# A third raw place and five float32 places for the weight halves of a two-expert kernel

## The chip, the cores and the metric

The kernel runs on one core of one Trainium2 chip. The metric is the device time of one execution in microseconds (us).

## The reference

Three steps follow each other. An attention over q, k and v of 4 batches, 8 heads, 576 rows and 64 columns keeps, in each row of scores, only those within tau of the row's maximum, and softmaxes them. Its output, 2304 rows of 512, goes through a first expert, whose activation is a quotient of polynomials, and the result through a second one, whose activation is piecewise quadratic:

```
attn = softmax(where(scores >= max(scores) - tau, scores, -1e9))
x  = (attn @ v) as 2304 x 512
h  = x @ w_in                      # 512 x 2048
g  = (a0 + a1 h + a2 h^2 + a3 h^3) / (1 + |b0||h| + |b1| h^2 + 1e-6)
x  = g @ w_out                     # 2048 x 512
h  = x @ w2_in
g  = h if h >= 1, 0 if h <= -1, else (h + 1)^2 / 4
out = g @ w2_out
```

The four weight matrices are handed over as float64; q, k, v and the output are float32.

## The kernel before, in words

All large products are done in float16 with the operands split in a high and a low part (three matmuls for one product). The work goes batch by batch: attention of a batch, first expert (24 steps: 3 blocks of 192 rows x 8 chunks of 256 of the 2048 columns), second expert (24 steps), then the next batch. `at(when)` (L175) gives each piece of work a priority, lowest first; a scheduler with a simulated time line makes each engine's order from it, when the program is built. A tile's place (a pool's tag has so many) is given out in that schedule, and is free when the last reader of the tile in it is done.

**Weights.** Each expert has 8 chunks with 2 halves each (x = 0: 512 x 256 of w_in; x = 1: 256 x 512 of w_out), 32 halves in all; they are numbered here from 0 to 31 in program order, the first expert's from 0 to 15. `convert` (L233) handles one half:
- L241 loads the raw half, 1 MB of float64 seen as pairs of int32, on the SP queue into a tile with the tag "rw" (pool rp, 2 places).
- `as_float` (L220) builds the float32 half in a tile "wt" (N_WT = 3 places, 4 KB in a partition) with three passes on DVE, L228, L229 and L230.
- L253 makes Gram products of the half on PE, L254 and L188 find their maximum (with matmuls of L187 between), and L168 to L172 a power of two from it.
- `split` (L205) scales the float32 half on ACT (L217), casts it to float16 (L208, the high part) and subtracts on POOL in four pieces (L212, the low part). The subtraction is the last reader of the float32 half.

For the first expert the two parts go into the chunk's own tile "wc" (8 places), which stays for the first batch, and a copy into DRAM scratch (L265). For the second expert they go through a staging tile "wh" (N_WH = 2 places, 4 KB in a partition) into scratch (L270); load_chunk (L275) reads chunks back later. The first expert's halves are interleaved with the first batch's attention (L869 to L875), the second expert's have the priorities of steps -3 to 17 (WEIGHTS, L887). The first expert's constants need a maximum over all of its halves.

**Attention of the first batch** (`first_attention`, L619) works on 4 pairs of heads. `prep_pair` (L317) loads raw q and k of one pair into the tile "rqk" (pool rp, 1 place, 5 KB in a partition), squares it on ACT for a bound (L328), scales and splits it into the float16 tile "qk" (pool ap, 1 place, 4.5 KB in a partition; for the first batch L217, L208, L212, for the others L214 and L215), and transposes that by DMA (L343 or L350). All four pairs are prepared by about 97 us. The next pair that uses these two tiles is the first of batch 1 (`attention`, L461; priority of step 16.5 on). Its v (`prep_v`, L289) is loaded into "rw" tiles, L300 and L298.

SP carries nearly all DMAs, in the order of the schedule.

Of the kernel before, what the change touches and what calls it, by code (L numbers as in the profile page):

```python
# [11 lines left out]
I32 = mybir.dt.int32  # L12
BF16 = mybir.dt.bfloat16
AF = mybir.ActivationFunctionType
ALU = mybir.AluOpType
# [19 lines left out]
N_TEMP, N_POLY, N_WT, N_WH, N_GG, N_ROW, N_SC = 5, 3, 3, 2, 4, 3, 2  # L35


ATTENTION = {1: (18, 50), 2: (60, 100), 3: (108, 147)}
WEIGHTS = (0, 20)

# [2 lines left out]
def tile_attention_moe_moe2(  # L43
# [18 lines left out]
    V, A, G, T, Q = nc.vector, nc.scalar, nc.gpsimd, nc.tensor, nc.sync  # L62
    B, H, S, D = q.shape
    P = 128
# [4 lines left out]
    DM, DF = w1_in.shape  # L69
    KT = DM // P  # L70
    NCH = 8
    CF = DF // NCH
    NF = CF // P
# [5 lines left out]
    E = KT * CF  # L79
# [3 lines left out]
    rp = ctx.enter_context(tc.tile_pool(name="rp", bufs=2))  # L83
    ap = ctx.enter_context(tc.tile_pool(name="ap", bufs=2))
    xp = ctx.enter_context(tc.tile_pool(name="xp", bufs=1))
    mp = ctx.enter_context(tc.tile_pool(name="mp", bufs=2))
# [106 lines left out]
    wide = w1_in.dtype != F32  # L193
    words = 2 if wide else 1
# [22 lines left out]
            A.activation(src, src, AF.Copy, scale=scale)  # L217
            split(hi, lo, src)

    def as_float(raw, name):  # L220

        if not wide:
            return raw
        src = raw.rearrange("p (n w) -> p n w", w=2)
        t = mp.tile([P, E], I32, name="wt" + name, tag="wt", bufs=N_WT)
        V.tensor_scalar(t, src[:, :, 1], 0x07FFFFFF, 3, op0=ALU.bitwise_and, op1=ALU.logical_shift_left)  # L228
        V.scalar_tensor_tensor(t, src[:, :, 1], -0x40000000, t, op0=ALU.bitwise_and, op1=ALU.bitwise_or)  # L229
        V.scalar_tensor_tensor(t, src[:, :, 0], 29, t, op0=ALU.logical_shift_right, op1=ALU.bitwise_or)  # L230
        return t.bitcast(F32)

    def convert(m, i, x, dst, on_vector):  # L233

        if x == 0:
            raw = rp.tile([P, KT, CF * words], raw_type, name=f"rw{m}_{i}_0", tag="rw")
            src = w_in_dram[m][:, i * CF * words : (i + 1) * CF * words].rearrange("(kt p) f -> p kt f", p=P)
        else:
            raw = rp.tile([P, NF, DM * words], raw_type, name=f"rw{m}_{i}_1", tag="rw")
            src = w_out_dram[m][i * CF : (i + 1) * CF, :].rearrange("(f p) d -> p f d", p=P)  # L240
        Q.dma_start(raw, src)  # L241
        name = f"{m}_{i}_{x}"
        src = as_float(raw.rearrange("p a b -> p (a b)"), name)
        hi, lo = dst[:, 0:E], dst[:, E : 2 * E]
        columns = m == 0 and x == 0
        bound = gram[:, i : i + 1] if columns else small(1, "mb" + name)
# [711 lines left out]
```

## Time and profile before

| | us |
|---|---|
| median of 3 runs | 1245.84 |
| lowest, highest | 1241.46, 1250.6 |
| the profiled execution | 1242.5 |
| its span | 1240.7 |
| PE busy in it (matmuls) | 1091.9 (88%) |
| DVE busy | 977.1 (79%) |
| ACT busy | 842.9 (68%) |
| POOL busy | 543.0 (44%) |
| mean granted clock of PE | 0.959 |

PE is the matmul engine, PEld its weight load, DVE the vector engine, ACT the scalar engine, POOL GpSimd, SP the queue that issues DMAs. Times are counted from the start of the span. A name such as wt<-rw says that a tile wt is written from a tile rw; L228 is line 228. In a time line each row is start, duration, engine, line, operation, tiles and shapes, with the idle time of the engine before it and what ended that in brackets.

### The profile page before, as it was taken

The numbers are of one execution on the slowest core, as the hardware profiler recorded it, in microseconds if no ns is written. First come the engines' busy times: TensorE is split into PE (matmuls) and PEld (weight loads), VectorE is DVE, ScalarE is ACT, GpSimd is POOL, SyncE is SP. The second block draws the span as 40 slices with busy tenths as digits, with TensorE's granted clock in tenths as the row PEclk, the third lists the DMA queues.
The fourth block names the chain that finished last, engine by engine and source line by source line (L and its number), as shares of the span: only waits on it lengthen the run. The fifth ranks groups of instructions, "written<-read, shape, count | busy, mean of one in ns | idle before, by whom it ended". The sixth has DMA issues, their size and how long they took to land.

```text
span 1240.7 us, 31727 instructions
## 1 busy us (share of the span) xinstructions
PE 1091.9 (88%) x12618; PEld 984.5 (79%) x12618; DVE 977.1 (79%) x2353; ACT 842.9 (68%) x1533; POOL 543.0 (44%) x700
## 2 busy tenths in 40 slices
PE   2787788588799999999888998998899999999998
PEld 1444455488688888899788898998788989999997
DVE  7767887899997777799997776899996768896431
ACT  2477776779785677777875776887766767775332
POOL 3424545675673556421464555223563653222221
PEclk9797898799899999999999999999999999999999
DMA  7656676734447465923596539513993478007000
GB/s 209 230 169 217 218 258 205 240 116 120 108 136 234 68 125 116 249 73 92 144 238 131 110 69 245 140 49 68 243 192 69 86 167 221 14 1 259 16 14 27
DMA packets 220341, 176.40 MB, mean 142 GB/s; under 512 B 182048, under 2 KB 193312, under 8 KB 212000
## 3 DMA queue, kind: packets, MB, share of 16 engines
q1 hardware_dynamic: 220192, 174.36, 52.7%
q8 instruction: 99, 1.62, 0.5%
q14 instruction: 50, 0.41, 0.1%
HBM read 106.83 MB, written 21.50 MB: 103 GB/s over the span
## 4 chain that ended last, share of the span: by engine, by line
PE 35%; DVE 19%; DMA 9%; ACT 6%; POOL 6%; issue 6%; SPq 1%; DVEq 0%; ACTq 0%; POOLq 0%
PE ph L843 15%; PE acc L857 15%; DMA eT<-hl 7%; POOL hl L395 3%; DVE e L384 2%; PE pv L410 2%; DVE t L731 2%; DVE t L726 2%; DVE sc L422 2%; DVE t L737 1%; DMA qkT<-qk 1%; DVE t L728 1%; POOL gg L212 1%; DVE t L727 1%; ACT hl L392 1%
## 5 line engine op out<-in xcount | busy, mean ns | idle before, releaser
L857 PE MATMUL acc<-gg,wc 128*128 128x192 f16 x4608 | 427.6, 247 | 9.8 <-POOL gg L212 6.4
L843 PEld LDWEIGHTS <-wc 128*128 128x128 f16 x4608 | 389.8, 99 | 37.4 <-issue 20.8
L857 PEld LDWEIGHTS <-wc 128*128 128x128 f16 x4608 | 383.4, 98 | 13.3 <-issue 12.0
L212 POOL TENSOR_TENSOR gg<-t,gg 128x384 f16<-128x384 f32 x192 | 193.3, 1008 | 380.0 <-ACT gg L208 330.0
L843 PE MATMUL ph<-xT,wc 128*128 128x192 f16 x2304 | 220.2, 253 | 29.7 <-DVE t L728 21.2
L843 PE MATMUL ph<-yT,wc 128*128 128x192 f16 x2304 | 215.9, 247 | 1.0 <-DVE rk_f L160 0.6
L395 POOL TENSOR_TENSOR hl<-e,hl 128x256 f16<-128x256 f32 x216 | 154.3, 735 | 0.0
L208 ACT CAST gg<-t 128x384 f16<-128x384 f32 x192 | 97.0, 508 | 68.8 <-DVE t L790 34.7
L789 DVE SCALAR_TENSOR_TENSOR t<-t,c 128x384 f32<-128x384 f32 x96 | 64.0, 667 | 77.3 <-ACT t L788 77.0
L384 DVE SCALAR_TENSOR_TENSOR e<-sc,nt,e 128x576 f32<-128x576 f32 x108 | 96.2, 891 | 31.9 <-ACT e L383 31.3
L393 POOL TENSOR_TENSOR hl<-e,hl 128x64 f16<-128x64 f32 x108 | 43.3, 401 | 145.0 <-ACT hl L392 141.4
L788 ACT ACTIVATE t<-ph,c 128x384 f32<-128x384 f32 x96 | 64.0, 667 | 51.6 <-PE ph L843 51.2
L383 ACT ACTIVATE e<-sc,nt,con 128x576 f32<-128x576 f32 x108 | 93.4, 865 | 7.4 <-POOL hl L395 1.3
L410 PE MATMUL pv<-v,eT 128*128 128x65 f16 (+3 forms) x1680 | 70.1, 194 | 26.8 <-DMA eT<-hl 26.6
L422 DVE TENSOR_SCALAR_CACHE_REDUCE sc<-s 128x576 f32<-128x576 f32 x108 | 80.9, 749 | 13.5 <-PE s L377 12.7
L410 PEld LDWEIGHTS <-eT 128*128 128x128 f16 (+1 forms) x1680 | 62.2, 100 | 36.1 <-DMA eT<-hl 33.8
L724 ACT ACTIVATE t<-ph,sc 128x384 f32<-128x384 f32 x96 | 55.2, 575 | 51.5 <-PE ph L843 50.0
L392 ACT CAST hl<-e 128x576 f16<-128x576 f32 x108 | 72.0, 668 | 25.9 <-DVE e L384 25.3
L731 DVE SCALAR_TENSOR_TENSOR t<-t,ka,t 128x384 f32<-128x384 f32 x96 | 70.1, 730 | 11.1 <-ACT t L730 10.8
L729 ACT ACTIVATE t<-t,lc 128x384 f32<-128x384 f32 x96 | 67.9, 708 | 15.4 <-DVE t L726 15.0
L212 POOL TENSOR_TENSOR wc<-wt,wc 128x256 f16<-128x256 f32 x64 | 55.3, 897 | 46.1 <-ACT wc L208 46.1
L212 POOL TENSOR_TENSOR wh<-wt,wh 128x256 f16<-128x256 f32 x64 | 59.7, 961 | 33.0 <-ACT wh L208 28.9
(231 smaller groups left out, 1901.7 us busy)
## 6 DMA issues: line engine op xcount, KB each, us to landing
wc<-scratch SPq DMA_DIRECT2D x56, 1024.0 KB, 5.8
rw<-in_moe_w_in_dram SPq DMA_DIRECT2D x16, 1024.0 KB, 5.7
rw<-in_moe_w_out_dram SPq DMA_DIRECT2D x16, 1024.0 KB, 5.1
scratch<-wc SPq DMA_DIRECT2D x8, 1024.0 KB, 5.1
scratch<-wh SPq DMA_DIRECT2D x16, 512.0 KB, 3.6
rqk<-in_q_dram SPq DMA_DIRECT2D x16, 256.0 KB, 3.6
rqk<-in_k_dram SPq DMA_DIRECT2D x16, 256.0 KB, 3.0
kT<-qkT SPq DMA_DIRECT2D x28, 144.0 KB, 2.5
```

Of the source, the lines that this page charges most:

```text
L208: A.copy(hi, src)
L212: G.tensor_tensor(lo[:, p], src[:, p], hi[:, p], op=ALU.subtract)
L383: A.activation(e, s, AF.Exp, bias=nb, scale=con[:, 0:1])
L384: V.scalar_tensor_tensor(e, s, th, e, op0=ALU.is_ge, op1=ALU.mult)
L392: A.copy(hi, e)
L395: G.tensor_tensor(lo_w[:, p], e[:, whole][:, p], hi[:, whole][:, p], op=ALU.subtract)
L410: T.matmul(pv[rows, 0:w], eT[:, c, cols], vv[:, h * NT + x if x < NT else H * NT + h, at : at + w], start=(n == 0), stop=(n == len(blocks) ...
L422: V.tensor_scalar(s, banks[:, 0:S], 1.0, -LARGEST, op0=ALU.mult, op1=ALU.max, accum_out=mx)
L729: A.activation(r, u, AF.Ln, bias=lc[:, 1:2], scale=lc[:, 0:1])
L731: V.scalar_tensor_tensor(s, s, ka[:, 0:1], r, op0=ALU.add, op1=ALU.mult)
L843: last = T.matmul(ph[:, f, :], w[:, wx, kt, f * P : (f + 1) * P], rhs, start=(n == 0), stop=(n == 3 * KT - 1))
L857: T.matmul(dst, w[:, wx, f, d * P : (d + 1) * P], gg[:, gx, f, :], start=(i == 0 and f == 0 and n == 0 and d % 2 == 0), stop=(i == NCH - 1 ...
```

## The change

Halves 8, 11, 14, 17, 20, 23 and 26 (every third from 8 on, the set THIRD) are no longer loaded into "rw". Their raw data goes in two DMAs of 512 KB, the first half into a tile with the tag "rqk", the second into one with the tag "qk", one place each, as before. `as_float` makes its three passes over each of the two pieces.

The float32 halves are counted through; for the first expert the numbers 3 and 4 of every five (halves 3, 4, 8, 9, 13, 14) take a place of "wh" instead of "wt". The second expert's halves all use "wt", and "wh" for staging, as before.

```
+THIRD = {divmod(n, 2) for n in range(8, 28, 3)}
...
+    turn = [0]
+    def as_float(raws, name, first):
         if not wide:
-            return raw
-        src = raw.rearrange("p (n w) -> p n w", w=2)
-        t = mp.tile([P, E], I32, name="wt" + name, tag="wt", bufs=N_WT)
-        V.tensor_scalar(t, src[:, :, 1], 0x07FFFFFF, 3, op0=ALU.bitwise_and, op1=ALU.logical_shift_left)
-        V.scalar_tensor_tensor(t, src[:, :, 1], -0x40000000, t, op0=ALU.bitwise_and, op1=ALU.bitwise_or)
-        V.scalar_tensor_tensor(t, src[:, :, 0], 29, t, op0=ALU.logical_shift_right, op1=ALU.bitwise_or)
+            return raws[0].rearrange("p a b -> p (a b)")
+        n = turn[0] % (N_WT + N_WH)
+        turn[0] += 1
+        if first and n >= N_WT:
+            t = mp.tile([P, E], I32, name="wt" + name, tag="wh", bufs=N_WH)
+        else:
+            t = mp.tile([P, E], I32, name="wt" + name, tag="wt", bufs=N_WT)
+        at = 0
+        for raw in raws:
+            src = raw.rearrange("p a (n w) -> p (a n) w", w=2)
+            to = t[:, at : at + src.shape[1]]
+            at += src.shape[1]
+            V.tensor_scalar(to, src[:, :, 1], 0x07FFFFFF, 3, op0=ALU.bitwise_and, op1=ALU.logical_shift_left)
+            V.scalar_tensor_tensor(to, src[:, :, 1], -0x40000000, to, op0=ALU.bitwise_and, op1=ALU.bitwise_or)
+            V.scalar_tensor_tensor(to, src[:, :, 0], 29, to, op0=ALU.logical_shift_right, op1=ALU.bitwise_or)
         return t.bitcast(F32)
...
+    def load_raw(m, i, x):
...
+        name, a = f"{m}_{i}_{x}", src.shape[1]
+        if wide and (m * NCH + i, x) in THIRD:
+            raws = [pool.tile([P, a // 2, src.shape[2]], raw_type, name=f"r{tag}{name}", tag=tag, bufs=1)
+                    for pool, tag in ((rp, "rqk"), (ap, "qk"))]
+            for n, raw in enumerate(raws):
+                Q.dma_start(raw, src[:, n * a // 2 : (n + 1) * a // 2])
+            return raws
+        raw = rp.tile([P, a, src.shape[2]], raw_type, name=f"rw{name}", tag="rw")
         Q.dma_start(raw, src)
+        return [raw]
...
     def convert(m, i, x, dst, on_vector):
...
-        src = as_float(raw.rearrange("p a b -> p (a b)"), name)
+        src = as_float(load_raw(m, i, x), name, m == 0)
```

## Rows read from the trace of the kernel before

**Rows 1.** Windows: busy time by stage; us, engines with instructions, clock, DMA share, GB/s

```profile
0.00:100.00 100.00, 58.47 (x328) 34.30 (x329) 68.78 (x170) 53.76 (x87) 35.42 (x52) 0.87 0.69 202
100.00:240.00 140.00, 108.15 (x676) 71.85 (x675) 115.27 (x238) 99.41 (x154) 74.75 (x84) 0.84 0.65 228
240.00:360.00 120.00, 96.92 (x1065) 91.25 (x1064) 115.43 (x257) 100.90 (x185) 77.44 (x80) 0.92 0.39 111
360.00:1240.00 880.00, 828.33 (x10556) 787.13 (x10553) 677.64 (x1691) 588.79 (x1110) 355.41 (x487) 0.99 0.52 126
```

**Rows 2.** Waits, 240 to 360 us: engine, line, releaser, us in total, times, longest

```profile
PE ph L843 <- DVE t L728: 17.2, 8, 4.5
```

**Rows 3.** Windows, 240 to 360 us, only instructions on the float32 halves (wt)

```profile
240.00:360.00 120.00, 4.04 (x40) 3.24 (x40) 11.44 (x11) 11.01 (x10) 19.41 (x23) 0.92 0.39 111
```

**Rows 4.** Windows by stage, only line 229, the second pass of each half

```profile
100.00:240.00 140.00, 27.05 (x21) 0.84 0.65 228
240.00:360.00 120.00, 3.90 (x4) 0.92 0.39 111
```

**Rows 5.** Time line of DVE, 190 to 250 us, first passes of halves

```profile
192.03 0.69 DVE L228 TENSOR_SCALAR wt<-rw 128x1024 int32<-128x1024 int32 x1 [0.56 <-POOL wh L212]
...
205.91 0.69 DVE L228 TENSOR_SCALAR wt<-rw 128x1024 int32<-128x1024 int32 x1 [1.37 <-POOL wh L212]
...
211.56 0.69 DVE L228 TENSOR_SCALAR wt<-rw 128x1024 int32<-128x1024 int32 x1 [0.80 <-POOL wh L212]
```

**Rows 6.** Time line of POOL, 190 to 250 us, subtractions of two halves

```profile
201.62 4.25 POOL L212 TENSOR_TENSOR wh<-wt,wh 128x256 f16<-128x256 f32 x4 [2.83 <-ACT wh L208]
208.29 3.24 POOL L212 TENSOR_TENSOR wh<-wt,wh 128x256 f16<-128x256 f32 x4 [2.42 <-ACT wh L208]
```

**Rows 7.** Time line of DVE, 50 to 130 us

```profile
68.80 0.70 DVE L228 TENSOR_SCALAR wt<-rw 128x1024 int32<-128x1024 int32 x1
...
72.02 2.32 DVE L230 SCALAR_TENSOR_TENSOR wt<-rw,wt 128x1024 int32<-128x1024 int32 x1
...
89.66 0.29 DVE L188 TENSOR_REDUCE mw<-pmmw 128x1 f32<-128x128 f32 x1 [0.49 <-PE pmmw L187]
89.98 0.15 DVE L168 TENSOR_SCALAR f_w<-mw 128x1 int32<-128x1 int32 x1
...
99.55 1.14 DVE L228 TENSOR_SCALAR wt<-rw 128x1024 int32<-128x1024 int32 x1 [0.56 <-POOL wc L212]
```

**Rows 8.** Time line of the SP queue, 60 to 105 us

```profile
66.56 0.37 SPq L241 DMA_DIRECT2D rw<-in_moe_w_in_dram  x1
...
93.29 1.30 SPq L350 DMA_TRANSPOSE kT<-qk  x1
94.79 0.43 SPq L321 DMA_DIRECT2D rqk<-in_q_dram  x1
```

**Rows 9.** Tile rw, 90 to 300 us: ns of one, min/median/max, first and last start

```profile
L228 DVE TENSOR_SCALAR wt<-rw x24: 677/688/1145, 99.6 to 268.7; 128x1024 int32<-128x1024 int32 x24
...
L230 DVE SCALAR_TENSOR_TENSOR wt<-rw,wt x24: 1209/1220/1686, 102.3 to 276.7; 128x1024 int32<-128x1024 int32 x24
```

**Rows 10.** Windows 80 to 100 and 100 to 160 us, columns as in rows 1

```profile
80.00:100.00 20.00, 13.51 (x101) 8.75 (x102) 10.55 (x39) 17.06 (x30) 7.10 (x7) 0.80 0.51 134
100.00:160.00 60.00, 48.35 (x302) 31.14 (x301) 52.11 (x99) 41.58 (x67) 31.64 (x36) 0.84 0.65 231
```

**Rows 11.** Time line of ACT: first pair of batch 1, square and scaling

```profile
101.67 0.67 ACT L328 ACTIVATE qk<-rqk 128x576 f16<-128x576 f32 x1
...
285.82 1.44 ACT L214 ACTIVATE qk<-rqk,qkr_s 128x576 f16<-128x576 f32 x2
```

**Rows 12.** Time line of PE, 80 to 100 us: Gram products and maximum of one half

```profile
88.00 0.62 PE L253 MATMUL pg<-wt 128*128 128x128 bf16 x8 [0.38 <-DVE mw L188]
89.13 0.49 PE L187 MATMUL pmmw<-ident,gram 128*128 128x128 f32 x2 [0.52 <-DVE gram L254]
```

**Rows 13.** Time line of PE, 230 to 245 us: the first expert's first matmuls

```profile
234.44 0.48 PE L843 MATMUL ph<-xT,wc 128*128 128x192 f16 x2 [4.38 <-ACT xT L613]
```

More of the change, by code (lines that the diff above doesn't have):

```diff
@@ L218, in split @@
             split(hi, lo, src)
-    def as_float(raw, name):
+    turn = [0]
+    def as_float(raws, name, first):
         if not wide:
-            return raw
-        src = raw.rearrange("p (n w) -> p n w", w=2)
-        t = mp.tile([P, E], I32, name="wt" + name, tag="wt", bufs=N_WT)
-        V.tensor_scalar(t, src[:, :, 1], 0x07FFFFFF, 3, op0=ALU.bitwise_and, op1=ALU.logical_shift_left)
-        V.scalar_tensor_tensor(t, src[:, :, 1], -0x40000000, t, op0=ALU.bitwise_and, op1=ALU.bitwise_or)
-        V.scalar_tensor_tensor(t, src[:, :, 0], 29, t, op0=ALU.logical_shift_right, op1=ALU.bitwise_or)
+            return raws[0].rearrange("p a b -> p (a b)")
[13 more added lines that the diff above has]
+            V.scalar_tensor_tensor(to, src[:, :, 0], 29, to, op0=ALU.logical_shift_right, op1=ALU.bitwise_or)
@@ L231, in as_float @@
         return t.bitcast(F32)
-    def convert(m, i, x, dst, on_vector):
+    def load_raw(m, i, x):
         if x == 0:
-            raw = rp.tile([P, KT, CF * words], raw_type, name=f"rw{m}_{i}_0", tag="rw")
             src = w_in_dram[m][:, i * CF * words : (i + 1) * CF * words].rearrange("(kt p) f -> p kt f", p=P)
         else:
-            raw = rp.tile([P, NF, DM * words], raw_type, name=f"rw{m}_{i}_1", tag="rw")
             src = w_out_dram[m][i * CF : (i + 1) * CF, :].rearrange("(f p) d -> p f d", p=P)
+        name, a = f"{m}_{i}_{x}", src.shape[1]
[6 more added lines that the diff above has]
+        raw = rp.tile([P, a, src.shape[2]], raw_type, name=f"rw{name}", tag="rw")
@@ L241, in convert @@
         Q.dma_start(raw, src)
+        return [raw]
+    def convert(m, i, x, dst, on_vector):
         name = f"{m}_{i}_{x}"
-        src = as_float(raw.rearrange("p a b -> p (a b)"), name)
+        src = as_float(load_raw(m, i, x), name, m == 0)
         hi, lo = dst[:, 0:E], dst[:, E : 2 * E]
```

## The prediction

> **What bounds the kernel now.** I began with busy time by stage [rows 1]. From 360 us on PE is busy 828 of 880 us; nothing of the change is at work there. Three stages stand before it: the start up to 100 us, the first attention with the weights from 100 to 240, and from 240 to 360 the first expert's first batch, with the last weights and the second attention beside it. In the last of these DVE is busy 115.4 of 120 us while PE idles 23.1 us. The waits of that stretch say the same: PE's largest wait is for DVE's polynomial step, 17.2 us in 8 waits [rows 2]. So DVE bounds 240 to 360, and what of its work goes elsewhere comes back as PE time, up to those 23 us. Part of it is weight conversion: 11.44 us of the three passes that turn a raw half into float32 are done there [rows 3].
>
> Then: why aren't the weights done sooner? Of the 32 halves' second passes 21 fall between 100 and 240 us and 4 (one of them cut by the edge) behind [rows 4]: one half per 140/21 = 6.7 us. What paces them is read from DVE and POOL side by side in the second expert's part [rows 5, 6]. POOL ends its subtractions at 201.62 + 4.25 = 205.87, and DVE begins the next half at 205.91; POOL ends at 208.29 + 3.24 = 211.53, DVE begins at 211.56. Each time DVE had sat idle for POOL. The subtraction is the last reader of the float32 half, so it is the float32 place that comes free. One half holds its place from DVE's 192.03 to POOL's 211.53, which is 19.5 us (half 21); three places give 19.5/3 = 6.5 us per half, the observed pace. The raw halves wait for a float32 place, not the other way round. In the first expert's part it is alike: half 7's passes begin at 68.80 and end at 74.3, and half 8's, loaded from 66.56 on [rows 8], begin only at 99.55, released by POOL [rows 7].
>
> **Part 1: five float32 places for the first expert.** Nothing is computed more or less. Six halves (3, 4, 8, 9, 13, 14) take one of the two half-size staging places, which the second expert's halves need only when the first expert's are done. With five places the bound on the pace falls to 19.5/5 = 3.9 us, and DVE is the next limit. One half costs it 0.69 + 1.22 + 1.22 = 3.13 us in passes [rows 9], two reductions like the one at 89.66 and three short operations of 0.15 us [rows 7]: 3.13 + 0.58 + 0.45 = 4.2 us. What can be gained is DVE's idle time: 9.45 us from 80 to 100, where half 9 can now be converted, and 60 - 52.1 = 7.9 us from 100 to 160 [rows 10]. Lower end: nothing of it is usable, 0 halves ahead. Upper end: 3.1 us of passes for a first half in the hole and 7.9/4.2 = 1.9 halves behind it, about 2.9 ahead. I take half the idle time behind 100 us and half a half from the hole, 1 + 0.5 = 1.5 halves: each half has a serial chain through PE, DVE, ACT and POOL, so not every idle microsecond can be filled.
>
> **Part 2: a third raw place (halves 8, 11, 14, 17, 20, 23, 26).** The q/k raw tile and the q/k float16 tile each take half of such a raw half. Half 8 can't be loaded at 66.56 any more: the float16 tile is read by the fourth pair's transposes, the last issued at 93.29 [rows 8]. With some 3 us for that to land and 5 for the load, half 8 lands near 103 instead of 72. But half 8 was converted only at 99.55 anyway, and halves 9 and 10 move up in the two ordinary raw places: cost about 0, up to +4 us of lead if halves 9 and 10 don't fill the gap. For the second expert a third raw place buys nothing by itself, since there the three float32 places stay and the raw halves already stand ready (row at 205.91: DVE waits for POOL and for no DMA). Gain 0. If it also hid a late load somewhere, it would be worth at most the one wait of 0.56 to 1.37 us that a half shows [rows 5].
>
> The price of the split: three passes become six, 7 halves x 3 = 21 more DVE instructions at about 0.15 us fixed each, 3.2 us, and 7 more DMA issues of 0.37 us on SP (row at 66.56 [rows 8]), which carries weights alone in that stretch. All seven are converted before 240, where DVE idles 140 - 115.3 = 24.7 us: hidden, 0; 3.2 us if that cover is gone.
>
> **What is moved.** Before, the raw q and k of the second attention's first pair were issued at 94.79, at once behind the fourth pair [rows 8]; ACT squared them at 101.67, and the tiles then lay waiting until the scaling at 285.82 [rows 11]. Now they can start only when half 26 has been converted, some 215 to 220 us by the pace. Load, square, maximum and root need about 15 us, so 235 comes before 286 with 50 us to spare: 0. The two squares (0.86 us each with their read-out) go from ACT's slack to a busier stretch; ACT is no bound there (100.9 of 120). Behind these DMAs on SP stand scratch writes and the v loads, which wait for raw places of their own. In the other direction the cost is open: it could be a gain below nothing too, as ACT loses 1.7 us near 101, in the hole that the weights now use.
>
> **The sum.** A lead of 1.5 halves at the end of the first expert is kept through the second, whose pace is set by the float32 places: 1.5 x 6.6 = 10 us sooner. In DVE work that leaves 240 to 360: 1.5 x 4.2 = -6.3 us, all of it within the 23.1 us that PE idles there. Against it: 1.5 halves more on PE before 240, 0.62 us of Gram products and 0.49 us for the maximum each [rows 12], 1.1 x 1.5 = +1.7 us onto the first attention, whose PE is busy 108 of 140 us at a mean granted clock of 0.84, so partly at the lower of its two levels (1.2 and 2.4 GHz) [rows 1]. That each of these 1.7 us delays the first expert is the dear end; the cheap one is 0, and I take the dear one. Split 0, move 0. Net -4.6 us. The profiled execution took 1242.5 us (span 1240.7 and 1.8 around it) and would come to 1237.9. It stands 3.3 us below the median of the three runs shown, 1245.84, so for a median I say 1245.8 - 4.6 = **1241 us**.
>
> **Rivals.** (A) *The weights get out of the way altogether.* The upper end of part 1, 2.9 halves, leaves almost nothing of the 11.44 us of passes and of some 3 us of small work after 240: about -14 us, less 2.9 x 1.1 = 3.2 on PE: -11; the loads of the second attention's v, which take the weights' raw places, come earlier as well; its rows could then fill some of the other 23.1 - 14 = 9 us of PE's idle time, half of it say: 1245.8 - 11 = 1235, with the v loads 1231. For it: the exactness with which place and pass follow each other [rows 5, 6]. Against it: DVE is at 87% from 100 to 160 and there is not much to fill. Chance 0.22.
>
> (B) *The lead is eaten by POOL.* The same four subtractions took 3.24 us in one half and 4.25 us in another [rows 6], the longer beside DVE's passes. If denser passes make all of them 4.25, the place is held 1.0 us longer, a third of that per half, 16 halves: 5.3 of the 10 us of lead are gone, and with the split's 0.47 us on 4 of those halves the sum is about -2: 1244. The Trainium skill has a rule for this (SBUF — State Buffer, "Who interferes with whom"): a DVE instruction with two SBUF inputs and a GpSimd instruction that reads SBUF exclude each other for the whole of an instruction; two of the three passes have two SBUF inputs. By that rule the trace agrees in kind (4.25 against 3.24), not that it always happens. Chance 0.18.
>
> (C) *Slower: the second attention starts late.* The first pair's q and k are behind half 26 and, on SP, behind scratch writes that wait for POOL. If their scaling comes after some 300 us instead of 285.82, the attention's first rows slip by 15 us out of a stretch in which PE has idle time to give, into one where it is at 94%: up to +15 us, 1261. It decides from the point where the loads are issued later than about 265 us. For it: the scheduler rebuilds the whole order. Against: 50 us to spare. Chance 0.12.
>
> (D) *It doesn't do what it says:* the second attention's pair takes the tiles at 95 us as before, and half 8 waits for them. The first expert needs all its halves for its bounds, so it can't begin at 234 [rows 13] if the pair is scaled only at 285.82: 52 us later, near 1298; about 1246 if it is scaled at once. Chance 0.03.
>
> **How the numbers follow.** The forecast has 0.45, with its own range 1235 to 1246 (0 to 2.9 halves, less PE). About 1% (12.5 us) is what a measurement of this kernel can tell from no change. Faster by more: the part of A with the v loads and a tail of the forecast, 0.22. Slower by more: most of C, D and a rebuilt order that falls badly, 0.14. Within 1%: 0.64. The range reaches from A's far side to short of C: 1228 to 1257.
>
> **What would show it.** Right: half 9's passes between 75 and 95 us; no wait of DVE for POOL before the first expert's passes between 100 and 160; in the second expert's part passes still starting at the end of POOL's subtractions, 6.5 us apart; the last half's third pass starting near 266 instead of 276.7 [rows 9]; less than 11.44 us of passes after 240 and less than 23 us of PE idle from 240 to 360. Wrong: halves of the second expert closer than 6 us (then raw places were the pace), the first matmul of the first expert later than 237 instead of 234.4, or q and k's scaling after 300.

## The result, and the profile after

The changed kernel takes 1262.06 us (median, 1260.77 to 1264.79) where the kernel before on the same chip takes 1248.22: a ratio of 1.0122, interval 1.0089 to 1.0155. A second measurement of the same pair gave 1.0139 (1.0093 to 1.0185). It is slower by about 1.2%, beyond the upper end of the forecast's range. The profiled execution took 1260.77 us, its span 1258.8, at a mean granted clock of 0.956.

Below are the windows by stage of the kernel after, columns as in [rows 1].

```profile
0.00:100.00 100.00, 58.79 (x326) 35.17 (x326) 69.90 (x171) 53.11 (x86) 37.85 (x53) 0.86 0.75 218
100.00:240.00 140.00, 105.58 (x661) 68.85 (x660) 114.31 (x256) 97.31 (x150) 68.56 (x82) 0.86 0.64 221
240.00:360.00 120.00, 92.96 (x1009) 86.43 (x1010) 116.97 (x248) 99.09 (x181) 80.57 (x83) 0.90 0.40 106
360.00:1240.00 880.00, 824.46 (x10475) 781.77 (x10474) 682.09 (x1701) 589.27 (x1114) 356.34 (x482) 0.99 0.53 126
```

From 240 to 360 us PE does less than before, 92.96 us against 96.92, though DVE does more. The stretch in front of it shows where PE lost its place. Two windows of the same kernel, to be read against the 48.35 us of [rows 10]:

```profile
100.00:140.00 40.00, 33.05 (x195) 20.76 (x195) 32.16 (x59) 22.94 (x39) 14.70 (x16) 0.84 0.56 194
140.00:160.00 20.00, 9.61 (x55) 6.33 (x55) 19.99 (x50) 11.94 (x19) 12.57 (x14) 0.58 0.71 236
```

From 140 to 160 DVE is busy all 20 us and PE only 9.61; the two windows add up to 42.66 us of PE. What DVE does there, in its time line of the kernel after (the operations on tiles of 128x9 are the row maximum of the third pair of heads, six steps of which each needs the one before):

```profile
143.14 0.36 DVE L571 TENSOR_TENSOR mx<-mx 128x9 f32<-128x9 f32 x1
143.50 0.69 DVE L240 TENSOR_SCALAR wt<-rw 128x1024 int32<-128x1024 int32 x1
144.12 0.75 DVE L629 SCALAR_TENSOR_TENSOR d<-d,rd 128x576 f32<-128x576 f32 x1
...
144.85 0.17 DVE L574 TENSOR_SCALAR pcs<-mx 128x9 f16<-128x9 f32 x1
144.92 1.22 DVE L241 SCALAR_TENSOR_TENSOR wt<-rw,wt 128x1024 int32<-128x1024 int32 x1
146.05 0.28 DVE L275 TENSOR_REDUCE mb<-pg 128x1 f32<-128x128 f32 x1
146.25 1.02 DVE L630 SCALAR_TENSOR_TENSOR x<-x,d 128x576 f32<-128x576 f32 x1
147.20 0.14 DVE L172 TENSOR_SCALAR f_w<-f_w 128x1 f32<-128x1 f32 x1
147.26 0.57 DVE L576 SCALAR_TENSOR_TENSOR mx<-pcs,mx 128x9 f32<-128x9 f16 x1
147.75 1.21 DVE L242 SCALAR_TENSOR_TENSOR wt<-rw,wt 128x1024 int32<-128x1024 int32 x1
...
149.15 0.37 DVE L574 TENSOR_SCALAR pcs<-mx 128x9 f16<-128x9 f32 x1
149.44 1.56 DVE L635 SCALAR_TENSOR_TENSOR xT<-x,v_s,xT 128x192 f16<-128x192 f32 x3
150.92 0.68 DVE L240 TENSOR_SCALAR wt<-rw 128x1024 int32<-128x1024 int32 x1
...
151.58 0.57 DVE L576 SCALAR_TENSOR_TENSOR mx<-pcs,mx 128x9 f32<-128x9 f16 x1
...
152.41 1.43 DVE L241 SCALAR_TENSOR_TENSOR wt<-rw,wt 128x1024 int32<-128x1024 int32 x1
...
153.82 0.57 DVE L574 TENSOR_SCALAR pcs<-mx 128x9 f16<-128x9 f32 x1
```

The six steps take from 143.14 to 154.39, 11.3 us. In the kernel before they took from 137.53 to 142.84, 5.3 us, with one first pass of a half between them. These are the first step, that pass and the last step in DVE's time line of before:

```profile
137.53 0.64 DVE L550 TENSOR_TENSOR mx<-mx 128x9 f32<-128x9 f32 x1
...
140.93 0.68 DVE L228 TENSOR_SCALAR wt<-rw 128x1024 int32<-128x1024 int32 x1
...
142.19 0.65 DVE L553 TENSOR_SCALAR pcs<-mx 128x9 f16<-128x9 f32 x1
```

In the kernel after, all three passes of half 15 and two of half 16 stand between the steps, beside the divide of the second pair (L628 to L630) and its transposed output (L635). The step at 147.26 had its input ready when the one at 144.85 ended; it waits only because four instructions stand ahead of it in DVE's queue. The Trainium skill says of this (PSUM — Partial Sum Buffer, "Engine vs sequencer instructions") that VectorE's queue is strictly first in, first out. The rows agree: each step starts at the end of what stands before it, within 0.1 us.

The attention that follows slips with it. This is PE's first long run of first-expert matmuls in the time line of before:

```profile
236.31 4.64 PE L843 MATMUL ph<-xT,wc 128*128 128x192 f16 x28 [1.38 <-DVE xT L614]
```

And this is the long run in the kernel after, with the short run ahead of it, which answers to [rows 13]. The row of [rows 13] is not literally the first expert's first: a few matmuls of the same line come sooner in both traces (nine of them at 226.37 before and at 238.57 after).

```profile
245.88 0.48 PE L864 MATMUL ph<-xT,wc 128*128 128x192 f16 x2 [4.30 <-ACT xT L634]
247.74 2.56 PE L864 MATMUL ph<-xT,wc 128*128 128x192 f16 x15 [1.38 <-DVE xT L635]
```

The weights themselves did get ahead. The third pass of the last half ended at 276.71 + 1.21 = 277.92 us before; after, DVE's time line has

```profile
261.76 1.21 DVE L242 SCALAR_TENSOR_TENSOR wt<-rw,wt 128x1024 int32<-128x1024 int32 x1
```

that is at 262.97, 15 us sooner. From here on the kernels are compared by these marks, read as starts from the time lines of PE and ACT: the last of the casts that end the third and the fourth pair's row maximum (mrow), the first long run of first-expert matmuls, and the cast that ends the first expert's third block of batch 0, its first block of batch 1 (the 7th block in order), its first block of batch 2 (the 13th), and the last block of all. Each row of the table is one profiled execution. The two of before differ by 3.5 us at the first run and by 11.5 at the end, so smaller differences between kernels with one profile each show nothing by themselves.

```
us                      mrow 3  mrow 4  first run  3rd    7th    13th    last
before                  146.5   188.4   236.3    387.9  562.6  820.9  1233.7
e15_before_again        150.1   191.8   239.8    392.2  569.7  830.2  1245.2
after                   159.8   202.0   247.7    397.4  574.3  841.2  1252.0
e14_after_again         158.7   200.4   245.8    395.6  571.3  836.4  1249.9
e1_places               154.7   198.7   251.8    403.6  572.3  832.9  1247.3
e2_raw                  147.7   198.6   243.1    391.1  567.4  828.1  1243.7
e3_raw_first            158.7   204.1   257.0    416.4  586.7  851.8  1263.4
e4_raw_second           156.9   197.0   246.5    390.6  571.1  829.6  1241.9
e5_gate                 151.1   195.2   240.5    401.7  567.1  826.5  1237.7
e6_gates                153.0   204.2   250.2    397.1  575.9  839.3  1254.5
e7_links                161.5   204.9   259.9    407.7  584.8  844.3  1255.1
e8_before_gates         147.0   184.2   227.4    389.8  572.2  830.2  1242.1
e9_three_gates          153.8   193.9   236.3    400.6  571.3  842.0  1258.0
e10_raw_first_gates     155.5   195.2   245.6    404.3  579.3  846.9  1262.8
e11_places_gates        148.2   193.8   239.7    397.2  565.9  829.2  1241.9
e12_other_gates         162.3   197.9   240.0    388.2  567.6  827.9  1240.3
e13_late_weights        146.3   188.2   236.2    385.3  566.2  828.5  1243.2
e17_places_gates        148.3   189.2   234.8    389.8  570.5  832.0  1245.6
```

### The profile page after: what moved, and what is told of

Read it like the earlier page. It is cut to its first block, busy times and chain, and to the rows that moved or that the text cites. A ratio compares the mean times of both kernels' runs of the same rounds, so it can differ in the third digit from the quotient of the medians.

```text
span 1258.8 us, 31782 instructions
## 1 busy us (share of the span) xinstructions
PE 1095.0 (87%) x12618; PEld 984.7 (78%) x12618; DVE 984.7 (78%) x2374; ACT 842.5 (67%) x1533; POOL 545.2 (43%) x700
## 4 chain that ended last, share of the span: by engine, by line
PE 36%; DVE 24%; DMA 8%; issue 5%; ACT 4%; POOL 4%; SPq 1%; DVEq 0%; ACTq 0%; POOLq 0%
PE acc L878 15%; PE ph L864 15%; DMA eT<-hl 6%; DVE t L752 2%; POOL hl L416 2%; DVE e L405 2%; DVE t L747 2%; PE pv L431 2%; DVE t L758 2%; DVE sc L443 2%; DVE t L749 2%; DVE t L748 2%; DVE t L757 1%; DMA qkT<-qk 1%; ACT hl L413 1%
## 5 line engine op out<-in xcount | busy, mean ns | idle before, releaser
L878 PEld LDWEIGHTS <-wc 128*128 128x128 f16 x4608 | 384.1, 98 | 11.5 <-issue 9.8
L864 PE MATMUL ph<-xT,wc 128*128 128x192 f16 x2304 | 216.9, 251 | 20.1 <-DVE t L749 12.5
L416 POOL TENSOR_TENSOR hl<-e,hl 128x256 f16<-128x256 f32 x216 | 158.0, 752 | 0.0
L443 DVE TENSOR_SCALAR_CACHE_REDUCE sc<-s 128x576 f32<-128x576 f32 x108 | 80.8, 748 | 10.9 <-PE s L398 10.3
L750 ACT ACTIVATE t<-t,lc 128x384 f32<-128x384 f32 x96 | 67.8, 708 | 23.1 <-DVE t L747 22.8
L752 DVE SCALAR_TENSOR_TENSOR t<-t,ka,t 128x384 f32<-128x384 f32 x96 | 70.8, 738 | 10.9 <-ACT t L751 10.4
L397 PE MATMUL s<-qkT 128*128 128x512 f16 (+1 forms) x240 | 63.7, 291 | 13.4 <-DVE sc L443 13.4
```

Source lines behind the costliest of these rows:

```text
L416: G.tensor_tensor(lo_w[:, p], e[:, whole][:, p], hi[:, whole][:, p], op=ALU.subtract)
L443: V.tensor_scalar(s, banks[:, 0:S], 1.0, -LARGEST, op0=ALU.mult, op1=ALU.max, accum_out=mx)
L750: A.activation(r, u, AF.Ln, bias=lc[:, 1:2], scale=lc[:, 0:1])
L752: V.scalar_tensor_tensor(s, s, ka[:, 0:1], r, op0=ALU.add, op1=ALU.mult)
L864: last = T.matmul(ph[:, f, :], w[:, wx, kt, f * P : (f + 1) * P], rhs, start=(n == 0), stop=(n == 3 * KT - 1))
L878: T.matmul(dst, w[:, wx, f, d * P : (d + 1) * P], gg[:, gx, f, :], start=(i == 0 and f == 0 and n == 0 and d % 2 == 0), stop=(i == NCH - 1 ...
```

## The experiments

**Which part costs.** The kernel after, with only some halves in the third raw place, or without the five places.

```
-THIRD = {divmod(n, 2) for n in range(8, 28, 3)}
+THIRD = set()                                      # e1_places
+THIRD = {divmod(n, 2) for n in range(8, 16, 3)}    # e3_raw_first
+THIRD = {divmod(n, 2) for n in range(17, 28, 3)}   # e4_raw_second

-        if first and n >= N_WT:
+        if False:                                  # e2_raw
```

> Only the five float32 places; no half is loaded into the q/k tiles. Theory P (more float32 halves are ready at once, and their passes stand on DVE between the links of the first attention's serial chains): most of the loss stays, 1254 to 1262 us, and the first expert's first long run of matmuls starts at 243 us or later, against 236.3 before and 247.7 in the changed kernel. Theory R (the split raw halves, their 21 more passes and the late half 8 cause the loss): 1242 to 1249 us, first run of matmuls at 233 to 238.

> Only the third raw place (seven halves through the q/k tiles); three float32 places for all. Theory P: no loss, 1244 to 1251 us, first run of matmuls at 234 to 240. Theory R: 1256 to 1263 us, at 244 or later.

> Five places, and the q/k tiles only for the first expert's halves 8, 11 and 14. Theory P: as the changed kernel, 1256 to 1264 us, since what counts happens before 160 us. Theory R: about half of the loss, near 1254, as 9 of the 21 more passes are left. If the second expert's four halves alone did it: 1244 to 1250.

> Five places, and the q/k tiles only for the second expert's halves 17, 20, 23 and 26. Theory P: 1254 to 1262 us, as with the five places alone. Theory R: near 1254. A rebuilt order that falls by chance would scatter these four kernels over 1240 to 1262 without regard to the part that they contain.

Measured against the kernel before (1246.59 us): five places alone 1259.18, ratio 1.0104 (1.007 to 1.0139); the third raw place alone 1249.22, 1.0034 (1.0004 to 1.0064); five places with halves 8, 11 and 14 in the raw place 1270.29, 1.0176 (1.0146 to 1.0206); five places with halves 17 to 26 in it 1253.84, 1.0059 (1.0031 to 1.0086). The five places are the dear part, the split and the third raw place cost 0.3% by themselves. In the three builds with five places the third pair's mrow is at 154.7 to 158.7 us, in the one without at 147.7, next to before. There were misses: e3_raw_first is slower than any of its expectations, and e2_raw has the time that theory P expected but a first run at 243.1, behind P's 234 to 240. The parts don't add up, either: each build has its own order on every engine, and e3_raw_first, with fewer halves moved, is the slowest of all. A rebuilt order that falls by chance is not excluded by these four.

The chain's length is not all of it. In e1_places DVE's time line has, at the third pair,

```profile
144.89 1.22 DVE L241 SCALAR_TENSOR_TENSOR wt<-rw,wt 128x1024 int32<-128x1024 int32 x1
...
146.22 0.16 DVE L571 TENSOR_TENSOR mx<-mx 128x9 f32<-128x9 f32 x1
...
149.36 0.18 DVE L574 TENSOR_SCALAR pcs<-mx 128x9 f16<-128x9 f32 x1
```

so its chain takes 3.3 us with one pass inside (the fourth pair's takes 1.5 with none), shorter than in before, and yet the first run comes at 251.8. The chain begins late there, 8.7 and 5.1 us behind the two profiles of before, with the passes of half 16 and two of half 17 just ahead of it. In e4_raw_second the two chains take 3.8 and 2.8 us without a pass between links, and the first run is at 246.5. Both point to the attention's work on DVE as a whole as what the passes delay, of which the third pair's chain is the part that shows best in the kernel after; e11_places_gates and e12_other_gates below bear on it.

**The order on DVE.** A gate issues a half's passes behind a chosen instruction, so that the scheduler can't put them ahead of it; nothing else is fixed by hand. In e5_gate:

```
+    links, GATES = {}, {15: 2, 16: 2}
...
-        src = as_float(load_raw(m, i, x), name, m == 0)
+        behind = links.get(GATES.get((m * NCH + i) * 2 + x))
+        raws = load_raw(m, i, x)
+        with tc.issue_after(behind) if behind is not None else nullcontext():
+            src = as_float(raws, name, m == 0)
...
-            V.tensor_scalar(pcs[:, x], m, 1.0 / PIECES[x], None, op0=ALU.mult)
+            links[pr] = V.tensor_scalar(pcs[:, x], m, 1.0 / PIECES[x], None, op0=ALU.mult).ins
```

> The changed kernel, but the DVE passes of halves 15 and 16 are issued behind the last link of the third pair's row-maximum chain; nothing else is moved by hand. Theory P (passes that stand between the links of the first attention's serial DVE chains cost the time): the third pair's chain, 11.3 us long in the changed kernel, takes 7 us or less, its last mrow cast comes at 153 to 155 us instead of 159.83, the first long run of first-expert matmuls begins at 242 to 244 us instead of 247.74, the median is 1254 to 1259. Rival (the order as a whole fell badly, that chain is one symptom among many): the first long run stays within 1.5 us of 247.7 and the median at 1259 to 1264.

Measured: 1247.98 us against 1246.71, ratio 1.0007 (0.9976 to 1.0038). The interval holds 1, so no loss is left that these runs can tell, which is more than was expected. DVE's time line of e5_gate at the same place:

```profile
142.00 0.36 DVE L575 TENSOR_TENSOR mx<-mx 128x9 f32<-128x9 f32 x1
142.28 0.75 DVE L633 SCALAR_TENSOR_TENSOR d<-d,rd 128x576 f32<-128x576 f32 x1
...
143.02 0.16 DVE L578 TENSOR_SCALAR pcs<-mx 128x9 f16<-128x9 f32 x1
143.09 0.74 DVE L634 SCALAR_TENSOR_TENSOR x<-x,d 128x576 f32<-128x576 f32 x1
...
143.82 0.15 DVE L580 SCALAR_TENSOR_TENSOR mx<-pcs,mx 128x9 f32<-128x9 f16 x1
...
144.16 0.15 DVE L578 TENSOR_SCALAR pcs<-mx 128x9 f16<-128x9 f32 x1
144.34 0.17 DVE L580 SCALAR_TENSOR_TENSOR mx<-pcs,mx 128x9 f32<-128x9 f16 x1
144.55 0.63 DVE L578 TENSOR_SCALAR pcs<-mx 128x9 f16<-128x9 f32 x1
145.08 0.68 DVE L241 TENSOR_SCALAR wt<-rw 128x1024 int32<-128x1024 int32 x1
```

The chain now takes 145.18 - 142.00 = 3.2 us instead of 11.3, and the next half's first pass stands behind it. The first long run begins at 240.47. But the marks say that the first attention is one half of the recovery: against the mean of the two profiles of after, e5_gate is 6.3 us ahead at the first run, 5.7 at the 7th block, 12.3 at the 13th and 13.2 at the end. Some 6.6 us come back only between the 7th and the 13th block. That half is taken up below.

The next kernel gates halves 8, 9 and 10 as well, behind the last operation of the first pair's divide (their passes delayed it in the kernel after).

```
-    links, GATES = {}, {15: 2, 16: 2}
+    links, GATES = {}, {8: ("d", 0), 9: ("d", 0), 10: ("d", 0), 15: 2, 16: 2}
...
-        V.scalar_tensor_tensor(x, x, -1.0, d, op0=ALU.mult, op1=ALU.mult)
+        links["d", pr] = V.scalar_tensor_tensor(x, x, -1.0, d, op0=ALU.mult, op1=ALU.mult).ins
```

> As e5_gate, and the passes of halves 8, 9 and 10 are issued behind the last operation of the first pair's divide. Theory P: both places at which the changed kernel lost time are mended, the first long run of first-expert matmuls begins at 237 to 241 us, the median is 1246 to 1253, level with the kernel before or at most 0.5% above it. Rival (order as a whole): 1259 to 1264. A third possibility, that halves 8 to 10 are then late for the first expert's bounds: the first long run no earlier than in e5_gate, 1256 to 1262.

Measured: 1258.82 us, ratio 1.0103 (1.0066 to 1.014): a miss for the theory as expected here. The time line of DVE shows why; the passes have slipped into the next chain, the fourth pair's:

```profile
186.77 0.16 DVE L575 TENSOR_TENSOR mx<-mx 128x9 f32<-128x9 f32 x1
...
187.05 0.68 DVE L242 SCALAR_TENSOR_TENSOR wt<-rrqk,wt 128x512 int32<-128x512 int32 x1
187.65 1.15 DVE L242 SCALAR_TENSOR_TENSOR wt<-rqk,wt 128x512 int32<-128x512 int32 x1
188.72 0.64 DVE L578 TENSOR_SCALAR pcs<-mx 128x9 f16<-128x9 f32 x1
...
197.68 0.64 DVE L578 TENSOR_SCALAR pcs<-mx 128x9 f16<-128x9 f32 x1
```

That chain takes 11.6 us; its mrow is 9.0 us later than in e5_gate (204.2 against 195.2), and the first run 9.7 us later. So the first run is late for the same reason, at another place. The next kernel adds gates for halves 20 and 21 behind the fourth pair's chain:

```
-    links, GATES = {}, {8: ("d", 0), 9: ("d", 0), 10: ("d", 0), 15: 2, 16: 2}
+    links, GATES = {}, {8: ("d", 0), 9: ("d", 0), 10: ("d", 0), 15: 2, 16: 2, 20: 3, 21: 3}
```

> As e6_gates, and the passes of halves 20 and 21 are issued behind the last link of the fourth pair's row-maximum chain. Theory P says that e6_gates was slow because these two halves had slipped into that chain (186.77 to 198.3 us there, 185.65 to 188.43 in e5_gate). With them out, its last mrow cast comes at 192 to 197 us instead of 204.23, the first long run of first-expert matmuls at 238 to 243 us instead of 250.21, the median is 1243 to 1250. Rival (gates on halves 8 to 10 make the weights late, and that is what e6_gates paid for): the first long run stays behind 246 us or the median above 1254.

Its first run comes at 236.3 us, even sooner than expected, 14 us before e6_gates. Yet it took 1261.02 us, 1.0108 (1.0038 to 1.0179). At the 7th block 4.6 us are left of the 14, and then it needs 270.6 us from the 7th to the 13th block, where the kernel before needs 258.3 and 260.5 in its two profiles. So the first run speaks for the theory and the time for the rival. The rival's reason, late weights, stays open: the last half's third pass ends at 284.2 us here, 277.9 and 281.5 in the two profiles of before.

Theory Q in an expectation below is that weights later than in the kernel before cost time by themselves; e13_late_weights, further down, tries it. The same two gates were put into e3_raw_first (halves 15, 16 behind the third pair, 20, 21 behind the fourth), and into e1_places three (15 to 17 behind the third pair), then also half 20 behind the fourth.

```
+    links, GATES = {}, {15: 2, 16: 2, 20: 3, 21: 3}    # in e3_raw_first: e10_raw_first_gates
+    links, GATES = {}, {15: 2, 16: 2, 17: 2}           # in e1_places: e11_places_gates
+    links, GATES = {}, {15: 2, 16: 2, 17: 2, 20: 3}    # in e1_places: e17_places_gates
```

> As e3_raw_first (five places; only halves 8, 11 and 14 in the third raw place), and the passes of halves 15 and 16 are issued behind the third pair's last link, those of 20 and 21 behind the fourth pair's. Theory P: the two chains that held passes in e3_raw_first are free of them, the first long run of first-expert matmuls comes at 238 to 246 us instead of 256.99, the median falls from 1270 to 1246 to 1256. Rival (that build's order is bad as a whole): the median stays above 1262.

> As e1_places (five places, no third raw place), and the passes of halves 15, 16 and 17 are issued behind the third pair's last link. Theory P: that pair's last mrow cast comes at 149 to 152 us instead of 154.66; the fourth pair's chain still has a divide and one pass of half 20 between its links, so not all of the loss comes back: the first long run of first-expert matmuls at 241 to 247 us instead of 251.79, the median 1248 to 1255. Rival: 1257 to 1262 as without the gates.

> As e11_places_gates (five places, no third raw place, halves 15 to 17 behind the third pair's last link), and half 20 behind the fourth pair's last link, whose chain then holds only the third pair's divide. With theory P and Q together: the first long run of first-expert matmuls moves from 239.71 to 235 to 239 us, the last pass stays before 278, so the median is 1243 to 1250, at or a little below e11_places_gates. Rival (the order behind these gates decides more than the chain): above 1254.

In all three the first run comes when it was expected or sooner: 257.0 to 245.6, 251.8 to 239.7, and 234.8 us. The times follow it in one: e11_places_gates takes 1251.34 us, 1.0036 (1.0011 to 1.0062), where e1_places was at 1.0104. But e10_raw_first_gates takes 1266.97, 1.0139 (1.0063 to 1.0216), not certainly less than e3_raw_first, as its rival expected, and e17_places_gates 1253.85, 1.0069 (1.0036 to 1.0102), above what was expected and just short of its rival, though its first run is ahead of the kernel before.

A control has two halves gated too, but 20 and 21 behind the fourth pair, and leaves 15 and 16 where they were.

```
-    links, GATES = {}, {15: 2, 16: 2}
+    links, GATES = {}, {20: 3, 21: 3}                  # e12_other_gates
```

> The control: the changed kernel with two halves gated as in e5_gate, but 20 and 21 behind the fourth pair's last link, where the changed kernel's chain was already free of passes; halves 15 and 16 stay between the links of the third pair's. The order on DVE is another one from the fourth pair on. Theory P: the third pair's last mrow cast stays at 159 to 160 us, the first long run of first-expert matmuls comes no sooner than 244, the median is 1255 to 1262. Rival (any reshuffle behind a gate can bring e5_gate's time): 1246 to 1252.

The third pair's mrow stays late, at 162.3 us, some 2 us later than expected. But the fourth pair makes most of it good, its mrow comes at 197.9 and the first run at 240.0, as soon as in e5_gate and not at 244 or later: a miss for the theory as it was put. The median is 1254.62, 1.0061 (1.0028 to 1.0095), between after and e5_gate and between what theory and rival expected. From one mrow mark to the other DVE spends 10.49 us on passes here and 16.95 in after, and the stretch takes 35.6 us instead of 42.1. So an 11.3 us chain of the third pair is not lost for good; what counts for the first run is how much of the passes stands in front of the attention up to its end.

**The chain by itself.** The kernel before, with nothing of the change, and one extra DVE pass over a tile of zeros before each of five links of the third pair's chain:

```
+            last = V.scalar_tensor_tensor(extra, extra, m[:, 0:1], extra, op0=ALU.mult, op1=ALU.mult).ins
+            with tc.issue_after(last):
+                op()
```

> The kernel before, with five extra DVE passes over a 128x768 float32 tile, some 0.8 to 1 us each, one before each link of the third pair's row-maximum chain; nothing of the change. Theory P: the chain grows from 5.3 to 9.5 to 11 us and what follows slips with it, the first long run of first-expert matmuls from 236.3 to 240 to 244 us, the median is 4 to 8 us above the kernel before on the same chip. Rival (there is slack around the chain, so that its length does not matter): 0 to 1.5 us above.

Measured: 1269.14 us, 1.0167 (1.0102 to 1.0231), far over the expected price. DVE's time line shows that the dose was larger than meant:

```profile
139.13 0.65 DVE L550 TENSOR_TENSOR mx<-mx 128x9 f32<-128x9 f32 x1
...
139.81 1.38 DVE L560 SCALAR_TENSOR_TENSOR extra<-extra,mx 128x768 f32<-128x768 f32 x1
141.11 0.64 DVE L565 TENSOR_SCALAR pcs<-mx 128x9 f16<-128x9 f32 x1
...
156.33 0.16 DVE L565 TENSOR_SCALAR pcs<-mx 128x9 f16<-128x9 f32 x1
```

The chain takes 17.4 us: the five extra passes are 5.7 us of it, and the passes of halves 14 and 15 went into the gaps that they opened. That is 12 us more than before, and the first run is 20 to 24 us later than in the two profiles of before. The rival, that the chain's length does not matter, falls for this order; e12_other_gates shows that it is no rule. Nor is the dose pure: the first run slips by more than the chain grows, and the tile of zeros takes one of the five places of the tag "tp", which the attention's own tiles use.

**Is sooner better than before?** The kernel before, with gates of its own:

```
+    links, GATES = {}, {14: 2, 15: 2, 18: 3, 19: 3}    # e8_before_gates
```

> The kernel before, with the passes of halves 14 and 15 issued behind the last link of the third pair's row-maximum chain and those of halves 18 and 19 behind that of the fourth pair; nothing of the change. Theory P: even with three places some passes stand in these chains, the first long run of first-expert matmuls comes 2 to 5 us before 236.3 and the median is 3 to 6 us below the kernel before on the same chip. Rival (the chains do not matter, or later passes cost as much as they give): within 2 us of it or above.

The first long run comes at 227.4 us, 9 to 12 us sooner than in before, more than expected. The kernel is nevertheless slower: 1255.54 us, 1.0062 (1.0032 to 1.0092). The passes that were held back have to be done later. This is what the passes take from the first run to the end of the third block (windows, only instructions on wt, columns as in [rows 3]), first in before, then in after, then in e8_before_gates:

```profile
236.31:387.86 151.55, 4.04 (x40) 3.24 (x40) 14.64 (x13) 12.57 (x12) 21.39 (x24) 0.92 0.48 145
```

```profile
247.74:397.37 149.63, 2.22 (x24) 1.87 (x24) 8.25 (x7) 8.01 (x8) 13.69 (x17) 0.94 0.47 129
```

```profile
227.40:389.82 162.42, 5.33 (x56) 4.34 (x56) 26.34 (x20) 19.73 (x18) 34.21 (x36) 0.92 0.49 153
```

e8_before_gates has 11.7 us more of passes there than before, and needs 10.9 us longer for the stretch: in this pair the lead of the attention is handed back almost one to one. That is no fixed price of a pass. e5_gate has 15.47 us of passes from its first run to the third block, 0.8 more than before, and takes 161.2 us, 9.6 longer; DVE is busy 157.7 us in it, as more of the second attention is done there (16 of its score tiles pass through DVE, rows sc<-s and e<-sc,nt,e, against 7 in before; that is 26.7 us against 11.6). The length of the stretch goes with all of DVE's work in it, and the order decides what that is.

Whether late weights alone cost something was tried on the kernel before with the last two halves gated behind the second block's second chunk; the first attention is unaltered.

```
+    links, GATES = {}, {30: "0_0_1_1", 31: "0_0_1_1"}
...
-        V.scalar_tensor_tensor(s, s, ka[:, 0:1], r, op0=ALU.add, op1=ALU.mult)
+        links[name] = V.scalar_tensor_tensor(s, s, ka[:, 0:1], r, op0=ALU.add, op1=ALU.mult).ins
```

> The kernel before, with the passes of the last two halves, 30 and 31, issued behind the polynomial's last multiplication of the second block's second chunk (294.28 us in the trace of before; the last half's third pass stands at 276.71 there). The first attention is left as it is. Theory Q (there is a second limit beside the end of the first attention: weights later than in the kernel before make the start of the second expert and the second attention's loads late): the first long run of first-expert matmuls stays at 235 to 238 us, the last pass comes at 295 to 300, and the median is 5 to 12 us above before. Rival (only the end of the first attention counts): within 2 us of before.

Measured: 1253.91 us against 1244.26, 1.0066 (1.003 to 1.0102), within what was expected, so the rival falls; the last pass ends at 293.7. But the marks don't bear out the reason that was given: the first run is at 236.2, the 7th block at 566.2 and the last at 1243.2, and from the 7th on all lie between the two profiles of before. Where the time goes is open, and that late weights hold up the second expert was not shown.

**The second slip, and scatter.** Both kernels once more, unaltered.

> The changed kernel again, unaltered, for a second profile. If the first long run of first-expert matmuls (247.74 us) and the slip of the blocks between 600 and 820 us (5 to 8 us more than at 563 us) are the kernel's own, both come back within 2 us and the median is 1260 to 1264. If the second slip is scatter between executions, it changes while the first does not.

> The kernel before again, unaltered, for a second profile: the ratio's interval holds 1. The first long run of first-expert matmuls comes within 2 us of 236.31. Its first profile, at 1242.5 us, lay below the median of its runs; if the stretch behind 560 us is what scatters between executions, the difference to a slower profile lies there.

After: 1261.39 us, 1.0139; before: 1246.46, 1.0007 (0.9978 to 1.0037). The two profiles of after agree within 2 us at the first run, and take 267.0 and 265.1 us from the 7th to the 13th block. The two of before differ by 3.5 us at the first run (236.31 and 239.82), by 11.5 at the end, and take 258.3 and 260.5 us from the 7th to the 13th block. The first run of before moved by more than the 2 us expected, and 7.1 of the 11.5 us stand ahead of the 7th block already. The second slip, some 6.6 us in the means, came back in the second profile of after and is larger than the some 2 us by which two profiles of one kernel differ there; that speaks against scatter, with two profiles of each.

It may go with the order. 2.0 of the 6.6 us arise up to the ninth block and 4.6 between the ninth and the thirteenth, where batch 1's second expert and batch 2's attention share the engines. There DVE has 324 instructions in the kernel before. Their order is the same, one by one, in e2, e4, e5, e6 and e8, and but for the first two in e7; it is another one in after, e1, e3, e9 to e13 and e17. From the 7th to the 13th block the first six and the two profiles of before take 258.1 to 263.4 us, 259.8 in the mean; the others, with the two profiles of after, take 260.3 to 270.6, 264.3 in the mean. The two ranges overlap, and e1 (260.6) and e12 (260.3) have another order and take as long as the second profile of before (260.5), so another order is not slower as such. The scheduler works from a simulated time line, so what shifts early in it can change choices 400 us later. No run forced the one order on the other kernel: the cause of this half is argued from a comparison and not shown.

## Why the prediction was wrong

**The sum.** With the mean of two profiles of each kernel: the first long run slips by 246.76 - 238.07 = 8.7 us; the stretch from there to the third block gets 2.2 us shorter (151.9 to 149.7); 0.1 us is added up to the 7th block, 6.6 between the 7th and the 13th, and 1.7 are gained behind it: +11.5 us. (The medians are 13.8 and 17.1 us apart in the two measurements; what the profiles don't hold of it is open.) The forecast had +1.7, -6.3 and nothing behind 360 us: -4.6.

**The step that failed** is the term for the first attention in the sum: "1.5 halves more on PE before 240 ... +1.7 us onto the first attention". It counted what the earlier halves cost PE, and took their DVE work as idle time filled, at no cost. Part of that idle time lies in short waits of the attention's own work: what fills it can stand ahead of the attention's next step in a queue that keeps its order. The sign that the prediction itself had named, a first matmul of the first expert later than 237, is the one that came (245.9 instead of 234.4). That DVE's order does it is shown by the gates, which fix nothing but the place of a few passes (the scheduler's order behind them moves too): the first run comes back to 240.5 in e5_gate (halves 15 and 16) and to 240.0 in e12_other_gates (20 and 21), against 238.07 in the mean of before. Which passes cost most is not settled, since either pair of gates does it. The price was 8.7 us, not 1.7. The clue was in the rows used: part 1 took 52.1 of 60 us as 7.9 us to be had [rows 10] without asking what the 52 us were waiting for.

**The relief** was right in kind and wrong in its worth. From the first run to the third block the passes fell from 14.6 us to 8.25 and 8.74, that is by 6.2. That this is so near the forecast's 6.3 is luck: the forecast counted 1.5 halves with their small operations, and in its own window, 240 to 360 us, the passes fell only from 11.44 to 10.59 and PE's idle time rose from 23.1 to 27.0 us, against the sign that it had named. Only 2.2 us of time came of the 6.2, because DVE did not get less to do: it is busy 143.5 us in that stretch after and 142.5 before, as other work moved in (nine instead of seven of the second attention's score tiles, 3.9 us, the most of it). A gain was counted at par that wasn't.

**The lead** itself was larger than forecast, 17.5 us at the last half's third pass in the means (279.7 to 262.2) against 10. It was not there at the end of the first expert and then kept, as forecast: half 15 is converted only 3.8 us sooner (147.27 to 143.50). The rest comes in the second expert's part, where before's half 30 begins 18.4 us behind half 29 (243.99 to 262.43). With 17.5 us it is of rival A's size, but A's time did not come of it. Nor did it come from the hole at 75 to 95 us. DVE's time line after:

```profile
95.74 0.92 DVE L240 TENSOR_SCALAR wt<-rrqk 128x512 int32<-128x512 int32 x1 [1.68 <-DMA rrqk<-in_moe_w_in_dram]
96.58 0.68 DVE L240 TENSOR_SCALAR wt<-rw 128x1024 int32<-128x1024 int32 x1
...
100.00 1.22 DVE L628 SCALAR_TENSOR_TENSOR d<-d,rd 128x576 f32<-128x576 f32 x1
...
106.25 1.22 DVE L629 SCALAR_TENSOR_TENSOR d<-d,rd 128x576 f32<-128x576 f32 x1
...
110.54 0.75 DVE L630 SCALAR_TENSOR_TENSOR x<-x,d 128x576 f32<-128x576 f32 x1
```

Half 9 stood behind half 8 in the queue, and DVE waited 1.68 us for half 8's raw data, although half 9 (the second row) had long been loaded. Then halves 8, 9 and 10 came in one burst, and the first pair's divide, three operations, was drawn out over 11.3 us between them. Part 2's "halves 9 and 10 move up" held (96.58 and 98.92 instead of 104.48 and 110.98 us), but not into the hole. Nor was part 2's price 0: alone it takes 1.0034 (1.0004 to 1.0064) of the time before (e2_raw). The divide is not the reason there, it takes 3.0 us as in before; what slips is the fourth pair's mrow, to 198.6. And the two parts are not independent, though they were added up: without the third raw place half 8 is converted from 72.84 us on and half 9 from 86.47, in the hole as part 1 counted on it (e1_places).

**The pace** of the second expert was right: its passes start at 204.33, then eight halves on at 256.74, 6.55 us each. So rival B (POOL eats the lead) did not occur either, though four subtractions took between 2.56 and 4.52 us on POOL from 160 to 240. **The move of q and k** showed no cost, as said. ACT scales them sooner than in [rows 11], so rival C did not occur:

```profile
274.40 1.44 ACT L215 ACTIVATE qk<-rqk,qkr_s 128x576 f16<-128x576 f32 x2
```

The time landed near rival C's 1261 by another way. **The order behind 360 us** was called untouched: "nothing of the change is at work there". That was wrong by 6.6 us, if the comparison above is accepted; among the chances, a "rebuilt order that falls badly" was named, but it had no price.

## What to carry to other kernels

Before work is moved forward into an engine's idle time, look at which chain leaves it idle: on an engine that keeps its order, a filler can land ahead of the next link of a serial chain, which then waits for it. Count earlier work as free only where what it would overtake is not the stage's last wait, and test it with a gate on the order, which costs a few lines. When a scheduler rebuilds the order from a time line, compare the order in stages that the change doesn't touch as well.

## What the runs showed that was not expected

Two executions of one program can differ by 3.5 us at the first long run and by 11.5 at the end (span 1240.7 and 1252.1), so one profile of each kernel can mislead by as much as the change itself costs. And an early end of the first attention did not make a faster kernel: with the first run at 227.4, 234.8 and 236.3 us, e8_before_gates, e17_places_gates and e9_three_gates were all slower than the kernel before, by 0.6 to 1.1%. None of the versions tried beats it.
